# Six blocks of x transposed by DMA in place of TensorE, with a new order table, in a fused attention and MoE kernel

## The chip, the cores and the metric

The kernel runs on one core of one Trainium2 chip. The metric is the device time of one execution in microseconds (us), lower is better. Three runs of the kernel before gave 299.45, 299.85 and 300.24 us; the median is 299.85 us. A separate execution was taken by the hardware profiler; all lines of profiles and traces below come from such executions.

The engines are written as the profile writes them: PE is TensorE (PEld its loading of weights), DVE is VectorE, ACT is ScalarE, POOL is GpSimd, SP is SyncE. SP and POOL mostly issue DMAs here.

## The reference

Sliding-window attention with a linear bias by distance, for 8 batches, 8 heads, 576 positions and a head size of 64, and behind it a feed-forward layer with the activation h·cos(h):

```python
scores = scale * np.matmul(q, k.transpose(0, 1, 3, 2))
bias = slopes[:, None, None] * (-np.abs(rel))[None, :, :]
mask = (rel >= 0) & (rel < 128)
scores = np.where(mask, scores + bias[None], -1e9)
attn = softmax(scores)
attn_out = np.matmul(attn, v)
x = attn_out.transpose(0, 2, 1, 3).reshape(B * S, H * D)   # 4608 x 512
h = x @ w_in                                               # w_in 512 x 2048
out = (h * np.cos(h)) @ w_out                              # w_out 2048 x 512
```

All inputs and the output are float32. The kernel computes in 16-bit types and accumulates in PSUM in float32.

## The kernel before

**Units of attention.** A batch's 576 positions are cut into two groups of 256 (G = 0 and 1) and a tail of 64. A unit (b, pr, G) is batch b, head pair pr (0 to 3) and group G; a unit (b, 't') is the tail with all heads. That makes 9 units for a batch, 72 in all, and they run mostly in pairs. For a pair, `scores` puts q·k products on TensorE (lines 529 and 539), ScalarE takes the exponential (598), VectorE multiplies with the mask (623), `pv` multiplies with v on TensorE (640 to 656, with the sum of the weights as an additional column) and VectorE divides by that sum (694, 696) into one of eight buffers `xnats`, as 128 positions times two blocks of 128.

**x transposed.** The next layer needs x with features on partitions. There are two ways. `x_pe` (719) makes two TensorE transposes against the identity (742) into PSUM and one copy from there into `xT`, on ScalarE (752) or VectorE (753). `x_dma` (757) issues a DMA transpose on SP (768; 762 for a tail), from `xnats` into `xT`, without TensorE. `xT` is a ring of 2560 tokens.

**The layer behind it.** The 4608 tokens are cut into 9 chunks of 512. `moe1(c)` multiplies chunk c with w_in (782): for each of 16 column blocks four matmuls, kc = 0 to 3, each of which reads one head pair's rows of `xT`, so the block's first matmul reads pair 0 and its fourth pair 3. Cosine on ScalarE (787) and a product on VectorE (791) follow. The second product with w_out runs in seven-product (Strassen) form for most chunks, `product` at 1067, and the first one does so for the last chunks (876). Chunk 0 has its own form (975).

**Phases.** Phase c is `moe1(c)`, then some units of attention (8, 10, 10, 12, 14, 9 units in phases 0 to 5), then the second product of chunk c. Nine units run before phase 0. In time these overlap: TensorE gets attention's matmuls of phase 2 between the products of chunks 1 and 2, and directly behind them moe1 of chunk 3. Units of phase 2 are those of batch 3 and (4,0,0); the four units (3,0,0) to (3,3,0) hold tokens 1728 to 1983, in chunk 3. Phase 3 begins with (4,1,0) and (4,2,0), tokens 2304 to 2559, in chunk 4.

**Which way x takes.** In `attention`, line 1208:

```python
first = (S * u[0] + (512 if u[1] == "t" else 256 * u[2])) // CH
after.append((first > phase + 1 or g < XD.get(phase, 0), u, ub, n))
```

A unit goes by DMA when its first chunk lies beyond the next phase's, or when its index g within the phase (pairs 0, 2, 4, ...) is below `XD[phase]`. XD is on line 275. With `{4: 6}` the second condition adds nothing to the first, since phase 4's first six units are far ahead of their chunks.

**The order.** `op` collects every operation with what it reads and writes, and does not decide the order. `TABLE`, a packed string of two bytes for each operation, names the order of all operations, and `follow` (160) applies it, and picks the engine of those copies that may run on ScalarE or on VectorE. Each engine then runs its own operations strictly in that order, and `emit` (174) puts a semaphore wait before each operation that reads, or overwrites, what another engine or a DMA has not finished. So a wait at the head of an engine's queue holds everything behind it on that engine.

**Loads and queues.** POOL issues the loads of q and k (`load_nat`, 385, five DMAs for a batch and tensor) and of v (`load_v`, 375, five for a batch). SP issues the big DMA transposes of q and k (396, 399), those of x (762, 768) and the stores of the output (1095). q, k and v of batches 0 and 1 are handled differently: q and k of these go through TensorE transposes (`qk_transposes`, 483). At the start POOL also makes the identity matrix (421) and the table of distances for the mask.

Of the kernel before, what the change touches and what calls it, by code (L numbers as in the profile page):

```python
# [27 lines left out]


TABLE = (  # L30
    'c-nPV2Y6If7JmPfH!Wo*A%PHdEHqifjs=k}tV#(GFqBXPBn4$bu`FK_%_4*%1ObV(K#D*JSt&-E!h-'
    '0xDvPKfD@{Z`QYO7kX6D^JciMYzU|;fHUhcd1+;jf_Kj&N_3_w#jJy552L+3%Pc;zlP#H-yktj(-'
    'pEjqM{ck}PJwCrB3q-'
    '{9M;&d$5qHR9WADS}~;_2H1xbO#`q+wdtgon`B>6%HyG|f?3%VnDsdnr<5N0St5ZZ)?8zmXNGD<Zg2=y6N`U+Gy?'
    '$F$*GyJWJoN!r+3anTS_iMU&FrmJy)q1{k##U*rYHRJHq^Dy35b!Y@oPU}o$A?_9;n<O%5Xs0l2&{m^^1BgNm_9P'
    '~pqObs4C1TN&{Qy{6(86~%nA#%H5NW^O=4`d2vLnc~h(_}2&mQcz_^`@$G{b79x#rnLjt-93Hcj0-'
    'yv%|m2e+*e0cZK}!+72b)WUaJT8@pXD+fk0N6bOV1gB(Si4?NA5T2-'
    '!JB(zEKr!Mj%{>;HUNYjab!Z7$qCql;L3G!CjefR+FFk(bw73vr<2ntCbb8MB)_5dQYyf6J%<J=0tY;ul(MgN&rc'
    'O0s&EiG$uIcm#Y~Vab;v#yqnaVrE7GY>V-A}Btqa`;P_Nv&jvF#{*7WM`>VMkre&#)Wy?uO_aV#gax-'
    'm{4=v5trFP6j>R?Tw2c0rY#J*M(j<PaOY>o)>#w^hUa2)xJ2kX>J~-'  # L40
    '#3SczLYEI#)13`0UMgZCvSU&r@KXVhQx8AYHOt^~S#t385v1pL)39f1&X4(!RY_VSn%~;N7Le~0Vt5k)3C!7qncH'
    'Sb_KKyP6<WQBL=(H{om`}^2hwehkBNkN1f6-'
    '=6Jf`#n1*9F&|{#~8ip5b`?XFO3>mnmKg4fqM&X#D2BXTu`vb#MxEL-'
    '2=FZh<=U!>)?uhVjo~ev?pC0h90j^d!W2#$W>Vg}3Lez;yMB~`dF58D5!*GHZ4bkokcrZJo8XMBIs3+J`c0!*&!='
    'cNak2M(+9t6%k<c;_TI5&xT-;_~SjMe)zLQ?kr-'
    '9G)}so_oZgT~!nS)>B%(>F{i(nL<%Kma6dPT_kIY8xqVGm@6sSZY)QY;}3kyZHF!JjrNbPWohF6A1kpQae^Jz>4Y'
    'nMq|4ag_#Z%abX$X0Qx{bdg5-'
    'w!C^Sy0wzSSv6YO*7!5g5KOZPW>L)jeqDWi^PVfHiNt_&bV&I7<#pb?el1f*R3lvbBscPqQM6(|M=#E!7MQtWiEo'
    '^$q8jetWg{{laSk`ID;w6<lHL!It@CI3ZRWxET-dy=6bdfZi^BN)-'
    'kx6rkxYh^Af7Y$CX%W0qP@nf!;+_cuy#JAV$$(>L5)aS8M@n1a32RRL3Yb{W0a`!VJ8|o4{JEnxs(L});p(&v8a9'  # L50
    'u_yO{KZHL$YuW?tu(Sy-'
    '!vCGTmAdZpg4wXLtycpkG<<E5@OtDZg=!_1h1+Njmjw*z0aL)7QnhFOPv(elHPlI>oe%EXgvk}suL+RHI+l!oPEe'
    'ttc)y)KY7q-'
    'GO9HpEp~!82*s>_!_J5TR{@5f%EL7h^Wh(4l4fbO%j~jd783&`#My06C4>3;+Is6L%3tT|^hYe#$tr1&iB&6{dwW'
    'wmj!;Baz_4=p8Jja_9ps>tY{=<;GUvOwSAXGq+K`;>!KNrH|ImXY(ASTzHFN^apdvpSj*r6^VK)$8H@P=`NPcPO&'
    'XkYSBhFw`irt0gqb!LQPqlVQC7VwU?z)4yP6n<)+6xUk=rH29r)HJ=#nkkufV0J5o_@v9wsQWd0@&P$WT0e*0vOC'
    'WIl=#9la*x}LDtWaQG=0xl2(#f%Kz3QWi+K|tR$xwKh#_K~ywPUk>V_~X988-'
    'dL$7M*|kTUzrMQ~>ttJm@GYT>9QFLiQ#JGHIu^Q5UX9joXGsV+1N~s5tf4rg&Z0t843@yK)VUZ;eO{vvf>bj#_<{'
    'E{YJE13lG{)N}UY3D6Y>lsCkRX4ja{$9_e$IQETy;j`zD56VwIGwJ{vRRhIkkY72;<?OL;WxyDsbjLJ`d?#gik4L'
    '%OwvOj>3X-Yk5pe`ia}jeHouYwjx-lYe?zUO*6w~{=z!E<7?VOdoJcyIBk3;YN22T&Udsl*?z2EoT*eN`VQ(2lOw'  # L60
    '$ie!%Cd#CND}y^H-5G~apWoVM#%(x$>q1=4UeA7@v$>FHVpXpRNz-`z1w9-2S&rNI|0<^yIkuIxJ1&2qr-'
    'yn-P&*BAkwbEg<YgZWM`B<Ux7!?;yxT0hEB9Poq9_H<xB+6$<+&1*V*jXQ=!i##UhbBC-HxJ9b4f>O5FQM$GVlYY'
    '0;EzOMeT$+Oi@ir?~G>em;QF`Fb7Uw0-'
    ')DSUv5QX5E;wvHsQX@ok50m+CO*%wR0XM0gH$JNq(o?|pd}rcrfU%@Ny^NS$EwY}9WNlRrb}CwAb0!CyUIkX8zeE'
    't`lBMNi5`Z9289jS-byN0#8`Z0-K46!6u51NJvfI*I<pVOKD}#Bep<(EjKAJ>#OvyA?}aT-'
    'Eb<QtZWG>gAiq@nZu|-Z>5YIIxXgTPJ-Qv8(%8OF{x~utj?J<T~4~q=Mu!G!`B%o{U^X7EYfMjy|cFw5l`KlR}P!'
    'Ka8_mW<8uzKs|eA|5Ic*_e7cdlcU3q+K^v!GU5I4-4igxj^A<ASLge=;<iQSZL!w7=WR?W#-'
    'vXhCLeN@7x(>g+{qRDABl6lLS<Fw>!h`LQKaFe(HMu)ipAva=P&;AW;|7_8}?>Xa&1&CWqRI3oTyJm0VHkMj~b-'
    'KU~R;VLVn(IO$x|2XD-#Cwa~YvoxGM@0FUnOnlZXB(9|3jhMQu{ARUV7(DVnyPJ@o)_f&pP-'
    '0v1&I@q5tK0fHEZqW2B6vpePz;Nsr3p!)OwvLraMQ%IB0%b!Fk8kvD!^ICX(d5SU`>)JBl;A)3x!^A~*gA1H!Njk'  # L70
    '9bb31AJ#9jLnSFn5nJP8V+>6WI*{{9$K=-'
    'Ii4(}ekB>9rlTbz8;dAV@$vsGY#Mm*p3)v9cI)0mEeyn;9Sk1Ej+_{IEB=6m(OWM%qp|L4FkV=POcUwRSz4?%tjO'
    '!EE7%nJVFo1y$1xLEKDW3+%V*`a_(LEi!<eA{Ja22J?)4@RI|7PRIIN8a6UkTIrQNx^0MmIX}Gdse33v8*ibI3(}'
    'Q6!`hQq7VFL0TWDyL%1z)LEb|Fqa2QJsRyz<9M$)jGC(Gyq6mu#GUiIyWiMn}lrw_vC^2CnX65Kq(JOA5auqsW#('
    'az6gPr;3Fs3vS*iFTO!lleCE-fW~K`s@;f-'
    'DuL7*vWwMFvwo)YDYK%Ys!&lL=}a$qa_Dqe_$j$%4|P%7Sk&C^p7|E-05OoaEoQU{w(_HKhuIl)N)0L6E?If-ndQ'
    'f>bOkomPRMj6=zXYB;2Fs8S$=8>KAS9bxj%$jo92RQykW$_h$ynL-'
    ';1n|B~0C{NjJ5M;#~HD{_qDyS92ASr8Q=(}$hf?wlN8Dh7U35CEE3Rb4eZHcVrLB=YO&ys+EVM&F9-'
    '>_E|awkyN8>TE$>Y^ZLfm%hXRv?#4)t*Y5EYzr4%5w1xWK3uw7gWYn<tfyI;9|8HRZ>;#t145fwkp%W<gb}oO8Vt'
    ';%~TDI391Zd3iT@kVuEmcuME+!AOkCeh?Xh408{MGRAGcvK=>2_;SOCz;Xi5FXBMh@##BcNK~)Hu608vNLvl*BDH'  # L80
# [15 lines left out]
class Plan:  # L96
# [63 lines left out]
    def follow(self, text):  # L160


        raw = zlib.decompress(base64.b85decode(text))
        n, at, self.order = len(raw) // 2, 0, []
        assert n == len(self.all)
        for lo, hi in zip(raw[:n], raw[n:]):
            at = (at + lo + 256 * hi) % 65536
# [85 lines left out]
def bass_alibi_sliding__then__act_gcu_kernel(  # L253
# [1071 lines left out]
```

## Time and profile before

| What | Value |
|---|---|
| Median of 3 runs (lowest, highest) | 299.85 us (299.45, 300.24) |
| The profiled execution's own time | 299.71 us |
| Its span, first to last instruction | 298.0 us |
| DVE TENSOR_TENSOR at 696 (normalising x) | 56 of 420 ns |
| DMA packets, data moved | 147729, 37.96 MB |
| HBM over the span | 155 GB/s |

How to read it: a line of instructions starts with its place in the kernel, then the engine and operation, what is written and read, and shapes. In a group's row, "xN \| busy, mean ns" gives the count, the busy time in us and the mean duration of one; that duration is from the start to the end of one instruction, and on TensorE several are in flight at a time, so the starts of neighbours in the timeline tell what one costs the stream. In a timeline's row the first two columns are the start and the busy time in us, and brackets hold the idle time before it and its releaser. Rows of waits hold the total, the count and the longest. Rows by stretches of time have the engines PE, PEld, DVE, ACT and POOL in this order, then TensorE's granted clock, the DMA share and GB/s. For DMAs, "to landing" is the time from the start of the issue to the last byte.

### The profile page before, as it was taken

What the parts mean: (1) busy time and instruction counts of PE and PEld (TensorE: products, weight loads), DVE (VectorE), ACT (ScalarE), POOL (GpSimd) and SP (SyncE); (2) the same over time, 40 slices, a digit from 0 to 9 for tenths busy, and PEclk for the clock granted to TensorE, in tenths of its full rate; (3) what the DMA queues carried; (4) which work ended last, traced back from release to release, by engine and by line L of the source; (5) the groups of instructions that cost most, each with busy time, mean ns of one, the idle gap of its engine ahead of it and who ended that gap; (6) DMA issues with size and microseconds to landing.
All of it is one profiled execution on the core that took longest, in us unless ns stands there. A gap on an engine that the chain in (4) does not pass through costs nothing.

```text
span 298.0 us, 7278 instructions
## 1 busy us (share of the span) xinstructions
PE 287.9 (97%) x2974; PEld 205.2 (69%) x2974; DVE 262.1 (88%) x522; ACT 222.1 (75%) x318; POOL 95.2 (32%) x122
## 2 busy tenths in 40 slices
PE   2899999999999999999999999999999999999996
PEld 2678845446874586458854788547768888888884
DVE  3879877599977999899999999999999999999972
ACT  5788878689757889688777878579778758778620
POOL 7997000599642303991195005000000000000000
PEclk9999999999999999999999999999999999999999
DMA  7999999999999994999999939973131400041033
GB/s 153 173 205 208 207 169 146 180 196 155 136 175 147 130 187 90 142 173 173 169 170 133 163 85 130 159 164 74 21 79 21 150 2 0 2 141 37 10 134 106
DMA packets 147729, 37.96 MB, mean 127 GB/s; under 512 B 133360, under 2 KB 146416, under 8 KB 147696
## 3 DMA queue, kind: packets, MB, share of 16 engines
q0 software_dynamic: 99344, 18.10, 79.7%
q1 hardware_dynamic: 48352, 19.41, 34.5%
q8 instruction: 23, 0.38, 0.5%
q14 instruction: 10, 0.08, 0.1%
HBM read 36.70 MB, written 9.44 MB: 155 GB/s over the span
## 4 chain that ended last, share of the span: by engine, by line
PE 94%; DVE 2%; POOL 1%; issue 1%; ACT 1%; POOLq 0%; DVEq 0%
PE ps L1067 33%; PE ps L782 24%; PE ps L876 11%; PE ps L539 5%; PE ps L975 5%; PE ps L1161 4%; PE ps L653 3%; PE ps L656 2%; PE ps L742 2%; PE ps L483 2%; PE ps L529 1%; DVE kt L501 1%; PE ps L640 1%; PE ps L642 1%; PE ps L1138 1%
## 5 line engine op out<-in xcount | busy, mean ns | idle before, releaser
L1067 PE MATMUL ps<-w_outb,gT 128*128 128x256 f16 x512 | 82.3, 273 | 0.0
L782 PE MATMUL ps<-xT,w_inb 128*128 128x512 f16 x336 | 82.2, 379 | 0.0
L787 ACT ACTIVATE cos<-ps,halfpi 128x512 f32<-128x512 f32 x84 | 54.9, 687 | 18.9 <-PE ps L782 13.9
L598 ACT ACTIVATE p<-ps 128x768 bf16<-128x768 f32 (+1 forms) x64 | 55.6, 915 | 11.5 <-PE ps L539 9.5
L791 DVE TENSOR_TENSOR gT<-ps,cos 128x512 f16<-128x512 f32 x84 | 54.5, 686 | 5.5 <-ACT cos L787 5.1
L1067 PEld LDWEIGHTS ps<-w_outb,gT 128*128 128x128 f16 x512 | 48.2, 98 | 12.5 <-issue 1.3
L782 PEld LDWEIGHTS ps<-xT,w_inb 128*128 128x128 f16 x336 | 31.7, 98 | 31.1 <-DVE gT L791 1.5
L375 POOL DMA_DIRECT2D vp<-in_v_dram x40 | 34.3, 892 | 53.1 <-PE ps L656 35.3
L1067 PE MATMUL ps<-wsum,gsum 128*128 128x256 f16 x256 | 38.5, 273 | 0.0
L623 DVE TENSOR_TENSOR p<-p,emask 128x768 bf16<-128x768 bf16 (+1 forms) x64 | 38.0, 615 | 0.3
L385 POOL DMA_DIRECT2D qnat<-in_q_dram x30 | 25.5, 918 | 23.9 <-DMA qt<-qnat 23.9
L1052 ACT ACTIVATE ob<-ps 128x512 f32<-128x512 f32 x33 | 19.6, 598 | 13.7 <-PE ps L1067 11.2
L385 POOL DMA_DIRECT2D knat<-in_k_dram x30 | 25.7, 948 | 9.3 <-DMA kt<-knat 7.0
L1067 PEld LDWEIGHTS ps<-wsum,gsum 128*128 128x128 f16 x256 | 23.2, 98 | 4.0 <-issue 0.5
L876 PE MATMUL ps<-xT,w_inb 128*128 128x256 f16 x132 | 24.8, 273 | 0.0
L696 DVE TENSOR_TENSOR xnats<-ps,rec 128x256 f16<-128x256 f32 x56 | 21.9, 420 | 0.5
L539 PE MATMUL ps<-qt,kt 64*128 64x128 bf16 (+1 forms) x320 | 20.1, 253 | 1.3 <-DVE kt L501 1.3
L653 PEld LDWEIGHTS ps<-vp,p 128*128 128x128 bf16 x256 | 16.0, 99 | 4.3 <-issue 1.0
L653 PE MATMUL ps<-vp,p 128*128 128x65 bf16 x256 | 18.9, 196 | 0.1
L1067 PE MATMUL ps<-wsum,gT 128*128 128x256 f16 x112 | 18.1, 273 | 0.0
L539 PEld LDWEIGHTS ps<-qt,kt 64*128 64x128 bf16 x320 | 11.9, 98 | 8.6 <-issue 3.6
L1161 PE MATMUL ps<-w_outb,gT 128*128 128x512 f16 x64 | 17.6, 380 | 0.0
(111 smaller groups left out, 478.0 us busy)
## 6 DMA issues: line engine op xcount, KB each, us to landing
out_dram<-ob SPq DMA_DIRECT2D x35, 256.0 KB, 2.7
vp<-in_v_dram POOLq DMA_DIRECT2D x32, 128.0 KB, 6.9
qnat<-in_q_dram POOLq DMA_DIRECT2D x24, 128.0 KB, 7.1
knat<-in_k_dram POOLq DMA_DIRECT2D x24, 128.0 KB, 10.8
w_inb<-in_moe_w_in_dram POOLq DMA_DIRECT2D x4, 512.0 KB, 10.5
w_outb<-in_moe_w_out_dram POOLq DMA_DIRECT2D x4, 512.0 KB, 21.8
gsum<-in_q_dram POOLq DMA_DIRECT2D x1, 576.0 KB, 15.5
gsum<-in_k_dram POOLq DMA_DIRECT2D x1, 576.0 KB, 17.6
```

The source lines that it names most:

```text
L375: op("pool", [lambda e, t=t, rows=rows: e.dma_start(vp[b % 2][0:rows, t, :, 0:64], v[b, :, 128 * t:128 * t + rows, :].rearrange("h p d -> ...
L385: fns.append(lambda e, t=t, rows=rows: e.dma_start(nat[which][b % 2][0:rows, t, :, :], src[b, :, 128 * t:128 * t + rows, :].rearrange("h p ...
L539: ins = e.matmul(ps[:, banks[x], c0:c1], keys_ap(b, x, pr, kc), query_ap(b, x, pr, qb, 128 * nb), start=c0 == 0 and (b, pr, G) not in seed ...
L598: op("act", lambda e: e.activation(P[i][:, :, 0:hi], src_[:, :, 0:hi], ACTF.Exp, scale=0.125), w=held + [("P", i)], occ=920 if G else 691, ...
L623: op("dve", lambda e: e.tensor_tensor(p, p, m, ALU.mult), r=[("EM", h0), ("EM", h1)] + ([] if G else [("EM2", h1)]), w=[("P", i)], occ=600 ...
L653: ins = e.matmul(o, P[i][:, x, d0:d0 + 128], V[:, kc, h, 0:65], start=True, stop=not two)
L782: op("pe", lambda e, kc=kc: e.matmul(ps[:, bank, :], w_in[:, kc, 128 * fc:128 * fc + 128], xT[:, kc, r0:r0 + CH], start=(kc == 0), stop=(k ...
L787: op("act", lambda e: e.activation(cosb[ci][:, :], ps[:, bank, :], ACTF.Sin, bias=halfpi[:, 0:1]), r=["halfpi"], w=[("B", bank), ("cos", c ...
L791: op("dve", lambda e: e.tensor_tensor(gT[gi][:, fc, :], ps[:, bank, :], cosb[ci][:, :], ALU.mult), r=[("cos", ci)], w=[("B", bank), ("g", ...
L876: op("pe", lambda e, i=i, kc=kc: e.matmul(ps[:, bank, 256 * i:256 * i + 256], left(kc, p0 + i), right(kc), start=(start and i == 0 and kc ...
L1067: op("pe", lambda e, t=t, p=p: e.matmul(ps[:, bank, 256 * t:256 * t + 256], left(p, slice(128 * t, 128 * t + 128)), right(p), start=(start ...
L1161: op("pe", lambda e, t=t, fc=fc, bank=bank: e.matmul(ps[:, bank, :], gT[gi][:, fc, 128 * t:128 * t + 128], w_out[:, fc, :], start=(fc == 0 ...
```

## The change

XD becomes `{2: 4, 3: 2, 4: 6}`: the first four units of phase 2, (3,0,0) to (3,3,0), and the first two of phase 3, (4,1,0) and (4,2,0), go by `x_dma` and not by `x_pe`. That removes twelve transposes on TensorE (70 become 58 at 742) and six copies from PSUM, and adds six DMA transposes on SP (29 become 35 at 768). `follow` no longer names ScalarE itself for copies that the table leaves on the first choice, but the operation's first engine, which is ScalarE for every copy that has a choice. The whole table is replaced, for the order of every engine; the new one has five lines fewer, so line numbers behind it are lower by five.

```diff
 TABLE = (
-    'c-nPV2Y6If7JmPfH!Wo*A%PHdEHqifjs=k}tV#(GFqBXPBn4$bu`FK_%_4*%1ObV(K#D*JSt&-E!h-'
...
+    'c-n1N33L=y7VX=6C*4`PlMs*?2^dC12atfuz$hx92#AC=>;Yl`L4qJ6OrmTV2M8dMB_t5SPC!R?9i79-9F-'
...
 )
@@ -167,7 +162,7 @@
             at = (at + lo + 256 * hi) % 65536
             o = self.all[at % 32768]
             if isinstance(o.fn, dict):
-                e = "dve" if at >= 32768 else "act"
+                e = "dve" if at >= 32768 else o.eng[0]
                 o.fn, o.eng = o.fn[e], (e,)
             self.order.append(o)
 
@@ -272,7 +267,7 @@
         KENG, DPEN, CENG = ("act",), 0, ("act", "dve")
-        JN, PRE2, SEEDN, XD, LORD = (5,), (), {}, {4: 6}, 0
+        JN, PRE2, SEEDN, XD, LORD = (5,), (), {}, {2: 4, 3: 2, 4: 6}, 0
         SDPRI, NH, LWPRI, G1, S4IN, SPLIT = 1, 2, 2, 1, True, True
```

What the new table moves beside the six units, as the order of the queues has it. On POOL the identity comes first and the distances later; and the five loads of q for batch 5, which were issued after a v load that waits for phase 2's pv, stand ahead of three v blocks of batch 3 (the fifth, the second and the first) and of the first v blocks of batch 4. On SP the four new transfers of phase 2 stand behind the k transposes of batch 4 and a store of chunk 1, and ahead of another store of chunk 1 and the q transposes of batch 5; those of phase 3 stand between stores of chunk 2 and the q transposes of batch 6. On TensorE the transposes of q and k for batch 0 are cut into smaller groups with scores between them. Of the copies that may run on either engine, VectorE gets 5 of those for x where it had 9, 8 of 16 for q and k where it had 9, and 4 of 35 for the output where it had 2.

More of the change, by code (lines that the diff above doesn't have):

```diff
@@ L30 @@
 TABLE = (
-    'c-nPV2Y6If7JmPfH!Wo*A%PHdEHqifjs=k}tV#(GFqBXPBn4$bu`FK_%_4*%1ObV(K#D*JSt&-E!h-'
[L32 to L80, printed above, removed]
@@ L81 @@
-    'GHNRFy;B3gs%n{7pj$fl+x7VWHhmHY6$LK<1t&5`BViq8BRfR0)!TR`@J<FZkbrVSDq@w=+*W79u-'
-    'AsdYv9Vyey(st|R(RU84Bg0wsI(4aO|@>6G)${!)5eW-e@5K<&=Z_fWO<s>k5KMFa_g&GrXJ7L|{Z-'
-    'kIjkN?mA0G*W>_y'
+    'c-n1N33L=y7VX=6C*4`PlMs*?2^dC12atfuz$hx92#AC=>;Yl`L4qJ6OrmTV2M8dMB_t5SPC!R?9i79-9F-'
+    '9~ZU<KgCkWX)ovl~u&->L|RW+4#cl}@gzyIES_r6yuv(c;dYJ6?b`E>9C+7wNTPS6;<MthV-)7oOYd$(x-'
+    'fZAl#xSH9Zs_ws~T}<uPUY{0SFId_-sc{<ULJMxCK)lqf4c*(5I@C<vl6C_Y7^9I?-'
+    '_R19YWvY*uA%9u`++u?+fmi6N`GG!9swM8y42z>I_qH|6HW^^)C?n_hZZI{;ko+s#i!5_-'
@@ new lines @@
+    'QmV}cZDZmO6x!kIxY{4rj=d)AivEHXz1Q*2jckl7C7P%!|mL%MLEY_*pGu3^-'
+    'q2QaTULs646TT{pn|qnGYSQ4xIz(WYy8L*0FkR5?tH?G{7`{w`qEX4b?fvG5#ztZb#Haz(=+nz`2R705{Nb8dF;6'
+    '_tP=<bE6w^rN2+0h>Sjb$J$5Zqsd1o@@e$E+{ipY?C7JDXwNx8Bbd~8)nh8hAGHoUE*M|3BmRPumKvGbg+cLWUOb'
+    'cUY1?&wHSHYQ)L*wVSN|SUKT?-'
+    '<(;q}lXA9h(WRG2MfE#h1A2PnqKpaKxqKEo#akCGiJ<wN7x1z}e9UMvZz>XC~dB6t!GLBTqJPl11Zd|qkg&PQ*Ml'
+    'F0cG~(cNvas(5wYnJCcD?&`q|x{{^!T0r=oj6u7q>ud#^?iTOgk{^_J3E2{)k>BG$vrf+(hIFTkDX7I;_K6>x)1)'
+    'DD=hEC$)E)`K}tqj%7{hA6{qcC}tpMgN=i|Y$F|>kY6nrENImbJW1-YT@o63Vyz3;SaUUkEstloxqz6a-'
@@ new lines @@
+    't@S~>KU*Z$YUnAk>@0)^)8FT^Y%+dP4(HE59l!b628I0Q=@?q7xD*ae*zx8fmni~{(AadEfAmd1Nwf}GpY49x>!H'
+    '!3yty8(0}(g+6m4FQEO?7Z7`!P9wv7uha2Rn(NZznr}OR4UiYdup;71adOO+Yp3tFW0=6O<$X*M~(^uAV9EfeGM7'
+    '=(1$mgdqN{8S@$HHUq7!J6n9fynJ&|@-Zk*Er~4$a;%`!I9U0|UDqp9@5biV^oVAIjR(=c&~+MM)-'
+    'nqLAK?rp@gl31hKIu-et}Yz~czI7Ey1reXSLNJ@h*<vua-'
+    '1F!WtF0y$~lHTL1UOPAyhim+*Fc2!O6n7#L9dW!K)X`K-'
+    'E1a?WU;X7D%hPcasm^*EN^(+ebs(xMTqf7gaF^TgV#?xeZj{cC0jJ^m#a=zIeknG=Q1JG44Z$$TWf*_7_vOJ?-'
+    '8m~fi3CY@Z#s~a9R(hmcu(^7!}HBPCvy8P#tTV1<~Pt{PADS4p{Fa=%;+%;kG6scO4l*cA+HtXEZXH1C`S_#-'
@@ new lines @@
+    '(LW73)mXRCY&G&7cZq@`Ak|=XmUkmo@Wy**ftB6HcMM+JECVc6%{YEJn`2Lr_z?CC_@Kx(^0IPCrS4_2k^A+<T%)'
+    ')a~fu5w&DWz0$Y}Bfi_C-'
+    ')i)$JfQqIL@iegLw<34>>KI*<&eR%%?Mr<;9S$UJM&7Pjbt!SEHEf!S%27yx?GGwVYYX3`zxo*DlXq`$#co4(K`8'
+    '-fXz7lx*btw_t@$yD%}QRX-zWkT<qY$OUmZUcKH6xmX|4orpc_s6-'
+    'eZxAWwWDf5$cobONj)wCUNCqSBDyU*VL|P5y?`rgnqUIZXwFOr2Vaweplvhf9FlD`R^-'
+    'U+c&E?8rhsac_i7vf&g`YZo-ISEO5fKW*OazwQ)UFGJ`3n0+`G5&Z}j|rpyz(^sf~2iR<S&NW%sv>3eCA{8XSZAo'
+    'B#Sp|{?dMT;o+hoUba_VKT<PSB`d8CdwsNw*i%%S^ZF*`0UyuU*}UAA94WPf~36egCM(a0`aZU2$`mT^mEE)O__E'
@@ new lines @@
+    'v0+6KNR{|vjOYAc67hJiYcq0u_ibO(jyo_{QL^Ll(kZew@;|^HB0ovRREC%59Yb>hP_Oe<PR3!;y)g-6u-'
+    '~hHO7ERNhrLAkwFN3|NWF+{Ays@j79TQqzbpNyeeuxC2(q^2{RjsOu~N?!K%ESGXVbIYe2M$v0hFhyM$yEUIjEpK'
+    '^F^898o=xMuneRIF=)91Up}G13}F1ojLkzbHlycA>N<HP#50avmvg;FTu2`F&g(1zO$AHQ^Ut3iL5zCi5_9UV=Yf'
+    'Ys(h<72`WUVZ`JDHhO(S{Ii98n@r*y7qefU=z`gCbpw|4zo>v`!pyP)bIvQl&cV%}Iy1<ahy>sRlUD`8%@YF(i8E'
+    'W+U_#P%q!YX?!dx@jY*k?q6G^6WA#rW;VSYTfEPJR)teo&fqfV@7Fw`>cJSP*(JqT=`Se?(&)Cyk*URA-'
+    '*{tcI&@>O-J9Oa0r^%5vhea#~pL`=w_BL-'
@@ new lines @@
+    'uv>`8L?F9PGpw(bW8k<L5V&V)3)P*2TxAAc0)V)6G}q;t3@Mw;=MVgf(G%;njB}8Giqn&wl=Fhxi-EzD^V;gqGmp'
+    'SHn(R+`n6i?v+hexu>Rpm8(K;n=hf$M^8eBidjsQ}J|k9OXWTz~bkd#48ciL8r)qZ&+SY!%irVN=doGUH=Mzmz=S'
+    '(_<G20gISU4Ow&z(D%^M1vbZO3o@Z6{vYH3f%ChvS{nEx?>v$F?mlZC{Mcy|cv<hjt9U`dI1*==TlKXHChxQT;Ga'
+    '&}`@em+#wC*hVE#_saH(#Yi6aKCE?%PLi}r#^U&h{Rb{jX*xj$PS>SXXMgZA9fb3fO3ksiK?(z^k#c*kNUhVOPNT'
+    'hH!5NGbho^d78%OM`9Pc{b>)JFpk7ystsK7LsTs$~E_O#}?E2vQFj@hb{Xnpnl+Ghy0EjgqUAG+1^Iqw)udHX=t$'
+    'JrD`S$0|W?tvM5eAyp^)9UQdPcZ6i=DTlnL~mltPE?V&%tf8*I)hYj<OPw7ytN&o?@2fUWRXmDZ)4>VH3S{hnUGu'
@@ new lines @@
+    '`0pz?~Z2rO*_`Nft>H9=@)k7`@n(5Vte(7U$i?@OIIx7CWJc*5nTCBet&_%^TESqle71I<jD0;`+D_UdxZ-'
+    'q9fR4T^*82{z}feG=eK$XuQG5@40Kc6xG>Vg7sgSarTDfr{J6IjRZ3kvug3#??JGyKmHu+BnHRADz%;RzOWO5%{;'
+    '?a)$%A0c}zxUnE#VN?}7J7iDA7qPIrfp5N)z)*!yBHRRdKtTxkN8ld>;Gq%6OA>hqQ1KiVHWSPO3mf)F$smM1CUd'
+    'F+Y2++mQkIgy8Tkb&#S9B$!z3`U@QoxaY1U*gh2seBmL-jaJyY7wF9;7A&%fN6pfx5vOKK$oZWcI+LJeZ7k|7wfB'
+    'mIP&3&SdNLIS_!ASv@$FgdDl62pN=$SieR#_6yXB_%_KRZQSylk%F$K#+?@!XAk^d9G!9B&%hzVG3uY3=5$Z)T0t'
+    'k83}2g$O|U(O#zllSwfgR6)H(G?jiY5Rgf$W&`ic<X_kXKB8bjdB#l*}5-'
@@ L84 @@
+    'BZtOs)%6q=J}SPU3e+%HepJDnf_^8iPVT@|x%$3JU2l2^LI(5o0p)GZ|a>QKAwdmsl`=a(YVC$|4FcV-iv_Nr98q'
+    'U1fn#RuMtMOGT%V!pfv%VRE7}`9`KvYC`^m$-HDNq9@5>2<kw=9wi^-YLcHI16Il)m4ai6@-'
+    '3mGzspFqAeXMZj7z*$f+-`5qBlsoY?z#kYLdVr+?6jCeG6s-EVO~iL?W#z5{=zMACbyp5jm9PjokyYPz7R&cM(Z-'
+    '5A#?Sa+rzXR|*Qt{~i$R`iv<%Y}n6`IS2%vSO&Pjx#j{(1(gCI$!nPiA5#`>MbVK|EheoQEHd@dvZ{z&rKpI~cqL'
+    '3`Owm+iy+^@YRRpr~UaVLX*)0Q?AO%;Yijb8`75QevUxDuNeyALUAO9a*5Fqg'
 )
```

## The prediction

> **What bounds the kernel now.** I read the page first (busy shares, granted clock, chain of waits), then the view of TensorE's waits, then its timeline where the change works.
>
> ```profile
> PE 287.9 (97%) x2974; PEld 205.2 (69%) x2974; DVE 262.1 (88%) x522; ACT 222.1 (75%) x318; POOL 95.2 (32%) x122
> PE 94%; DVE 2%; POOL 1%; issue 1%; ACT 1%; POOLq 0%; DVEq 0%
> core 0: 298.0 us, clock 1.000
> PE ps L483 <- POOL ident L421: 5.7, 1, 5.7
> PE ps L539 <- DVE kt L501: 1.3, 2, 0.9
> ```
>
> TensorE is busy 287.9 of 298.0 us and carries 94% of the chain that ended last, at a granted clock of 1.000. Its waits are two groups, 5.7 and 1.3 us, both before 14 us (rows below). From then on it always has a matmul in flight, so in that stretch only two things can move the end: work taken from its stream or put into it, and a new wait in that stream. VectorE (88%) and ScalarE (75%) have room.
>
> ```profile
> 5.70 1.92 PE L483 MATMUL ps<-ident,gsum 128*64 128x128 bf16 x32 [5.70 <-POOL ident L421]
> 8.50 0.82 PE L539 MATMUL ps<-qt,kt 64*128 64x256 bf16 x8 [0.88 <-DVE kt L501]
> 13.50 1.04 PE L539 MATMUL ps<-qt,kt 64*128 64x256 bf16 x12 [0.38 <-DVE kt L501]
> ```
>
> The profiled execution took 299.71 us for a span of 298.0, 1.7 us around it, and lies 0.14 us under the median of 299.85. I make the sum against 299.71 and set the result beside the median at the end.
>
> **What is removed from TensorE.** Each of the six units loses two transposes (line 742) and one copy from PSUM (752 on ScalarE or 753 on VectorE): 12 of 70 transposes go. The group's row says 230 ns for one, but that is how long one stays in the pipeline. What it costs the stream is the distance to the next start:
>
> ```profile
> L742 PE MATMUL ps<-ident,xnats 128*128 128x128 f16 x70 | 9.4, 230 | 0.0
> 113.84 0.28 PE L742 MATMUL ps<-ident,xnats 128*128 128x128 f16 x2
> 113.95 0.38 PE L1067 MATMUL ps<-wsum,gsum 128*128 128x256 f16 x2
> 114.17 0.28 PE L742 MATMUL ps<-ident,xnats 128*128 128x128 f16 x2
> 114.28 0.27 PE L1067 MATMUL ps<-wsum,gsum 128*128 128x256 f16 x1
> 111.10 0.39 PE L742 MATMUL ps<-ident,xnats 128*128 128x128 f16 x4
> 111.32 0.38 PE L1067 MATMUL ps<-wsum,gsum 128*128 128x256 f16 x2
> ```
>
> Two take 113.95 − 113.84 = 0.11 us and again 114.28 − 114.17 = 0.11; four take 111.32 − 111.10 = 0.22. So 55 ns each, and 12 × 0.055 = **0.66 us** leave the stream. By the row's 230 ns it would be 2.8 us; that is the far bound, and I take 0.66 because the neighbours' starts show it three times.
>
> The Trainium skill, "TensorE: Matmul & The Clock Gate", Part 4, gives about 275 ns for such a transpose in one kernel's context and puts most of it to access latency. By that the six units would give back 12 × 0.275 = 3.3 us. The trace agrees with it on the duration (230) and not on the price in a full pipeline (55). The same skill, "VectorE: DVE Perf Modes", Rules for kernel authors, advises against this change: it keeps a 128×128 transpose on TensorE where PSUM will do as a destination, with 390 ns against 1309 ns by DMA; here the issue row below (1247 ns for two blocks) is not TensorE's time, so the rule decides only if the landing is waited for.
>
> The six copies lost cost ScalarE or VectorE some 0.39 us each in the pipeline, but nothing waits there now that TensorE would notice, so I cost them at nothing (cover gone: less than 0.39 × 6 = 2.3 us to gain, all of it only if those engines bound a stretch, which the TensorE rows exclude after 14 us). The four or five other copies that change engine in the new table are covered by the same.
>
> ```profile
> L752 ACT ACTIVATE xT<-ps 128x256 f16<-128x256 f16 x27 | 9.6, 389 | 7.3 <-PE ps L742 6.1 <-PE ps L729 1.1
> ```
>
> **What is added.** Six more DMA transposes of x on SP (line 768), 29 become 35: units (3,0..3,0) in phase 2, (4,1,0) and (4,2,0) in phase 3. They differ from the 29: in the kernel before no unit goes by DMA whose tokens the very next phase reads, while these six are due in it. TensorE takes its work in order, so a late one stops all of it.
>
> ```profile
> L768 SPq DMA_TRANSPOSE xT<-xnats x9: 1169/1247/1391, 121.9 to 168.5; - x9
> DMA to landing us min/median/max: 3.0/5.8/7.6
> ...
> L768 SPq DMA_TRANSPOSE xT<-xnats x20: 1168/1247/2227, 173.6 to 223.8; - x20
> DMA to landing us min/median/max: 2.3/2.4/5.5
> ```
>
> SP needs 1.25 us to issue one. From issue to landing it is 3.0 to 7.6 us (median 5.8) while loads are in flight (120 to 170 us), and 2.3 to 5.5 (median 2.4) afterwards.
>
> The tightest is the fourth of phase 2. In the changed order, between the pv matmuls of (3,2,0) and (3,3,0) and the first matmul of chunk 3's moe1 that reads the fourth quarter of x (line 782), stand 38 products of line 1067, 3 of line 782, 32 pv, 8 transposes and two score blocks. Rows for their rates:
>
> ```profile
> 109.79 1.48 PE L1067 MATMUL ps<-wsum,gsum 128*128 128x256 f16 x12
> 111.64 0.62 PE L539 MATMUL ps<-qt,kt 64*128 64x256 bf16 x12
> 112.19 0.28 PE L1067 MATMUL ps<-wsum,gsum 128*128 128x256 f16 x1
> 112.38 0.19 PE L653 MATMUL ps<-vp,p 128*128 128x65 bf16 x1
> 112.86 1.15 PE L1067 MATMUL ps<-wsum,gsum 128*128 128x256 f16 x9
> 116.30 0.81 PE L782 MATMUL ps<-xT,w_inb 128*128 128x512 f16 x3
> 116.95 0.27 PE L742 MATMUL ps<-ident,xnats 128*128 128x128 f16 x2
> 110.28 0.76 DVE L696 TENSOR_TENSOR xnats<-ps,rec 128x256 f16<-128x256 f32 x2
> ```
>
> Twelve products take 111.10 − 109.79 = 1.31 us, 0.109 each; three of line 782 0.65; sixteen pv 112.86 − 112.38 = 0.48; a score block about 0.55 with 0.1 to enter it. Sum: 38 × 0.109 + 0.65 + 2 × 0.48 + 8 × 0.055 + 2 × 0.65 = 7.5 us. The pair's pv ends at 109.79 and its second normalised block at 110.28 + 0.76 = 111.04, 1.25 later; the third transfer is then issued, and the fourth 1.25 behind it, so 2.5 us after pv, with 0.1 for the hand-over. That leaves 7.5 − 2.6 = **4.9 us** for the fourth to land, about 5.8 for the third; the first two, a pair earlier, have 7 to 8.5. Against the quiet 2.4 it is ample; against the loaded 5.8 it lacks 0.9 us; against 7.6, 2.7 us. Which holds depends on what is in the DMA queues near 112 us:
>
> ```profile
> 108.00:112.00 4.00, 4.00 (x63) 3.29 (x62) 3.72 (x10) 3.76 (x8) 0.00 (x0) 1.00 1.33 230
> 112.00:116.00 4.00, 4.00 (x82) 3.11 (x77) 3.61 (x9) 3.54 (x6) 0.00 (x0) 1.00 0.03 10
> 95.30 4.19 POOL L385 DMA_DIRECT2D knat<-in_k_dram  x5 [7.03 <-DMA kt<-knat]
> 116.64 0.89 POOL L375 DMA_DIRECT2D vp<-in_v_dram  x1 [17.15 <-PE ps L656]
> 117.51 4.20 POOL L385 DMA_DIRECT2D qnat<-in_q_dram  x5
> 106.29 1.25 SPq L399 DMA_TRANSPOSE qt<-qnat  x1
> qnat<-in_q_dram POOLq DMA_DIRECT2D x24, 128.0 KB, 7.1
> ```
>
> In these windows (the last two columns are DMA share and GB/s) the queues work at 230 GB/s up to 112 and stand still, at 10 GB/s, from 112 to 116: just when the four would fly. But the new table also moves work there. The five loads of q that POOL issues at 117.51 are ahead of v's last blocks in the changed order, before 100 us: 4.5 × 128 KB = 576 KB more to drain, 2.5 us at 230 GB/s. The quiet begins near 114.5 in place of 112. The fourth transfer, issued near 113, meets some 1.5 us of backlog: an estimate of 2.4 + 1.5 = 3.9 us, inside its 4.9. So I take no wait, with bounds 0 and 2.7 us.
>
> The same move puts three blocks of v of batch 3 behind those q loads. Their bounds come from the v loads before 90 us:
>
> ```profile
> L375 POOL DMA_DIRECT2D vp<-in_v_dram x13: 707/920/972, 59.3 to 87.4; - x13
> DMA to landing us min/median/max: 5.4/6.9/15.5
> ```
>
> By their place in the order they are issued some 90 us into the span (an estimate from the rows of POOL) and land between 96 and 105.5; pv of batch 3 starts near 107. Taken: no wait, with a margin of 1.5 us at the slow end. In phase 3 the pair's pv runs near 137.5, two issues follow, and chunk 4 reads x some 11 us later, so even 7.6 us fits: nothing.
>
> On SP the four stand after the last big transposes of k (row at 106.29 for the last such issue before) and ahead of the next store and of q's transposes for batch 5. Those wait 5 us at most; q of batch 5 is first read in phase 3, 25 us on, and no output buffer is refilled before its store. Nothing.
>
> **The table.** Every engine's order is new. For the whole rest I count: the same matmuls, in the same phases; in steady state as many score blocks as before, so as many entries of 0.1 us. In the start-up the identity comes first on POOL, and the transposes of q and k are cut by score blocks earlier. What it can win are the rows of waits above: 1.3 us on kt, part of 5.7 on ident; what it can lose is of that size, as k and q are issued some 0.2 to 0.8 us later on their queues. Taken: 0, bounds −1.3 and +0.8. At the end the last chunk is bound by its matmuls in both orders: 0.
>
> **The sum**: −0.66 + 0 (copies) + 0 (landing) + 0 (v) + 0 (table) = −0.66: 299.05 by the profiled execution, 299.19 by the median. **Forecast 299.1 us.** About 0.3% (0.9 us) is what a measurement of this kernel tells from no change, and the forecast lies just inside that.
>
> **The rivals.**
>
> *The new table wins more than the transposes do.* The kt waits (1.3 us) sit where it re-cuts the start. If they go, the end is 299.71 − 0.66 − 1.3 = 297.7, half of them 298.4. For it: those are the only waits that TensorE has outside the first 5.7 us. Against: k's arrival, not the order, may set them.
>
> *The fourth landing is late* (slower). The moved q loads are still draining, the transfer takes the loaded 5.8 to 7.6 us, and the moe1 of chunk 3 stands at its fourth quarter: 0.9 to 2.7 us. It ends at 299.05 + 0.9 = 299.95 up to 301.8. The point: a landing over 4.9 + 0.66 = 5.6 us loses to the kernel before, over 6.5 us by more than 0.3%. For it: nine of nine transfers between 120 and 170 took 3.0 or more, half 5.8. Against: the 10 GB/s row.
>
> *Nothing shows.* The 0.66 us is given back in the start-up by q and k issued later (+0.8): 299.9.
>
> *A transpose costs its duration.* Twelve times 0.230 gives 296.9. Against it stand the three start distances. 3 in 100.
>
> **How the numbers follow.** The sum holds, 0.45, with 298.7 to 299.6 as its own range; two fifths of it fall under 298.95 with small gains of the table. The table wins more, 0.19, faster. Late landing, 0.22: 0.17 of it slower, 0.05 same. Nothing shows, 0.11: 0.05 same, 0.06 slower with a start that loses a little more. Duration, 0.03, faster. Faster 0.18 + 0.19 + 0.03 = 0.40; same 0.27 + 0.05 + 0.05 = 0.37; slower 0.23. The range goes from 298.1 (most of the table's gain) to 301.4 (a landing near 7.2 us).
>
> **What would show it.** In the profile after: 58 transposes on line 742 and 35 DMA transposes on line 768; TensorE's busy time lower by about 0.7; no wait of line 782 for x near 117 us (it would be listed with a DMA of xT as its releaser) and none of line 653 for v near 107; the landings of the four under 4.9 us; the waits at ident and kt about as long as now. The prediction is wrong if line 782 shows such a wait of 0.6 us or more, if the kt waits are gone, or if matmuls after 18 us start further apart than before.

## The result, and the profile after

| | before | changed |
|---|---|---|
| median, lowest to highest, 4 runs each | 299.79 us, 299.45 to 300.24 | 304.01 us, 302.89 to 306.63 |
| ratio, 95% interval | | 1.0147 [1.0119, 1.0174] |
| profiled execution, its span | 299.71 us, 298.0 us | 306.63 us, 304.9 us |

The changed kernel is 1.5% slower. Its profiled execution is also its slowest one, 2.6 us over the median, so what is read there is at the large end. Line numbers of the changed kernel, e1 and e8 are lower by five than before: pv's 653 is 648, the v loads' 375 is 370, the q loads' 385 is 380, x's transposes 742 are 737, x by DMA 768 is 763, moe1's 782 is 777. Those of e2, e3, e5, e6, e7 and e9 are lower by twelve (pv 641, v 363, x by DMA 756, moe1 770); e4 has those of before.

First the page's busy shares and its chain of waits:

```profile
PE 289.9 (95%) x2962; PEld 205.2 (67%) x2962; DVE 262.4 (86%) x519; ACT 220.5 (72%) x315; POOL 95.1 (31%) x122
PE 80%; DMA 12%; POOL 3%; SPq 2%; issue 1%; ACT 1%; DVE 1%; POOLq 0%; ACTq 0%
```

Then the view of TensorE's waits (total, times, longest), and the row of the transposes in the view of groups:

```profile
PE ps L478 <- DVE gsum L362: 5.7, 1, 5.7
PE ps L648 <- DMA vp<-in_v_dram: 4.3, 1, 4.3
PE ps L534 <- DVE kt L496: 0.9, 1, 0.9
PE ps L478 <- DMA gsum<-in_k_dram: 0.5, 1, 0.5
PE ps L534 <- DVE gT L786: 0.2, 1, 0.2
```

```profile
L737 PE MATMUL ps<-ident,xnats 128*128 128x128 f16 x58 | 8.1, 229 | 0.1
```

The twelve transposes are gone, and DMA has come into the chain that ended last, with 12%. One wait is new and large: pv for a load of v. TensorE's timeline shows its place:

```profile
107.83 0.50 PE L534 MATMUL ps<-qt,kt 64*128 64x256 bf16 x8
112.66 0.27 PE L648 MATMUL ps<-vp,p 128*128 128x65 bf16 x3 [4.33 <-DMA vp<-in_v_dram]
```

The windows (PE, PEld, DVE, ACT, POOL, then clock, DMA share, GB/s) show what followed:

```profile
108.00:112.00 4.00, 0.33 (x8) 0.10 (x4) 0.80 (x2) 1.88 (x3) 0.00 (x0) 1.00 1.88 155
112.00:114.00 2.00, 1.34 (x18) 1.13 (x19) 0.76 (x4) 0.00 (x0) 0.00 (x0) 0.84 1.84 218
114.00:116.00 2.00, 2.00 (x15) 1.22 (x14) 1.40 (x4) 0.00 (x0) 0.00 (x0) 0.50 2.43 155
116.00:118.00 2.00, 2.00 (x33) 1.60 (x28) 1.01 (x5) 1.22 (x2) 0.00 (x0) 0.81 2.33 167
```

TensorE stood for 4.33 us at the first pv of batch 3. When it went on, the granted clock fell to 0.50 and was back only after 116 us. Over the three windows from 112 to 118 us the missing shares, 0.16, 0.50 and 0.19 of 2 us each, come to 1.7 us. The profiled execution lost 306.63 − 299.71 = 6.92 us: 4.33 of waiting, 1.7 of clock, and some 1.5 left over, against 0.66 worked out as saved. The clock's part belongs to this execution: its mean granted clock was 0.994, while the other three show 1.000, 1.000 and 0.998 and took 2.3 to 3.7 us less. So hardly any of the median's loss of 4.2 us is clock.

Why v came late is seen on POOL's timeline:

```profile
77.86 1.97 POOL L370 DMA_DIRECT2D vp<-in_v_dram  x2
84.11 4.19 POOL L380 DMA_DIRECT2D qnat<-in_q_dram  x5 [4.29 <-DMA qt<-qnat]
88.26 4.24 POOL L370 DMA_DIRECT2D vp<-in_v_dram  x5
97.56 4.19 POOL L380 DMA_DIRECT2D knat<-in_k_dram  x5 [5.06 <-DMA kt<-knat]
```

and in the landings of its loads, by their lines, q from 84 to 89 us and v from 88 to 93 us:

```profile
L380 POOL DMA_DIRECT2D qnat<-in_q_dram x5: 722/883/903, 84.1 to 87.6; - x5
DMA to landing us min/median/max: 17.7/19.2/21.2
...
L370 POOL DMA_DIRECT2D vp<-in_v_dram x5: 728/938/950, 88.3 to 91.5; - x5
DMA to landing us min/median/max: 21.7/22.8/23.3
```

The first three of the five v blocks are those of batch 3. By the trace they were issued from 88.3 to 89.8 us, 18 us or more ahead of need (112.66 − 4.33 = 108.33), and landed 21.7 to 22.8 us later, the last at 112.6 us. In front of them stood the five q loads that the new table had moved forward, which land from 84.1 + 17.7 = 101.8 to 87.6 + 21.2 = 108.8 us: 1.75 us from one landing to the next. But the queue was long before these: the two v blocks issued near 78 us, ahead of the moved q loads, already took about 20 us:

```profile
L370 POOL DMA_DIRECT2D vp<-in_v_dram x2: 1082/1089/1096, 77.9 to 78.7; - x2
DMA to landing us min/median/max: 19.1/19.9/20.6
```

The transfers of x, which the prediction watched, were not waited for; no line of TensorE's waits names xT. They don't test its sum either, since TensorE came to them late. Near their use:

```profile
L763 SPq DMA_TRANSPOSE xT<-xnats x4: 1168/1245/2247, 113.9 to 120.4; - x4
DMA to landing us min/median/max: 2.3/4.3/5.9
```

### The profile page after: what moved, and what is told of

Its sections match the earlier page's. It is cut to its first block, busy times and chain, and to the rows that moved or that the text cites. A ratio compares the mean times of both kernels' runs of the same rounds, so it can differ in the third digit from the quotient of the medians.

```text
span 304.9 us, 7267 instructions
## 1 busy us (share of the span) xinstructions
PE 289.9 (95%) x2962; PEld 205.2 (67%) x2962; DVE 262.4 (86%) x519; ACT 220.5 (72%) x315; POOL 95.1 (31%) x122
## 4 chain that ended last, share of the span: by engine, by line
PE 80%; DMA 12%; POOL 3%; SPq 2%; issue 1%; ACT 1%; DVE 1%; POOLq 0%; ACTq 0%
PE ps L1062 28%; PE ps L777 19%; PE ps L871 11%; DMA vp<-in_v_dram 7%; PE ps L970 5%; PE ps L534 4%; PE ps L1156 4%; PE ps L648 3%; DMA qt<-qnat 3%; DMA gsum<-in_k_dram 2%; PE ps L651 2%; SPq L391 2%; POOL qnat L380 1%; PE ps L478 1%; PE ps L737 1%
## 5 line engine op out<-in xcount | busy, mean ns | idle before, releaser
L1062 PE MATMUL ps<-w_outb,gT 128*128 128x256 f16 x512 | 83.8, 275 | 0.0
L593 ACT ACTIVATE p<-ps 128x768 bf16<-128x768 f32 (+1 forms) x64 | 55.9, 915 | 17.5 <-PE ps L534 14.4
L1062 PE MATMUL ps<-wsum,gsum 128*128 128x256 f16 x256 | 40.1, 275 | 0.0
L1047 ACT ACTIVATE ob<-ps 128x512 f32<-128x512 f32 x31 | 18.4, 598 | 8.4 <-PE ps L1062 8.1
L1062 PE MATMUL ps<-wsum,gT 128*128 128x256 f16 x112 | 19.9, 273 | 0.0
```

The lines of the kernel that those rows point to most:

```text
L593: op("act", lambda e: e.activation(P[i][:, :, 0:hi], src_[:, :, 0:hi], ACTF.Exp, scale=0.125), w=held + [("P", i)], occ=920 if G else 691, ...
L1062: op("pe", lambda e, t=t, p=p: e.matmul(ps[:, bank, 256 * t:256 * t + 256], left(p, slice(128 * t, 128 * t + 128)), right(p), start=(start ...
```

## The experiments

There were three theories. V: the v blocks behind the moved q loads are the loss. X: transposing x by DMA just ahead of its use costs. T: the new order costs in many places. In the edits, `load(name, n)` is the n-th operation on a DMA semaphore, and `move` puts one operation directly behind another. Ratios are against the kernel before, run on the same chip.

| Run | ratio, 95% interval |
|---|---|
| changed kernel | 1.0147 [1.0119, 1.0174] |
| e1: changed, v ahead of the q loads | 1.0053 [1.0037, 1.0069] |
| e2: before, six x by DMA | 1.0012 [0.9999, 1.0024] |
| e3: changed order, six x by TensorE | 1.0118 [1.0085, 1.0152] |
| e4: before, two v loads late | 1.0224 [1.0193, 1.0254] |
| e5: before, four x of phase 2 by DMA | 0.9982 [0.9969, 0.9995] |
| e6: before, two x of phase 3 by DMA | 1.0019 [1.0005, 1.0034] |
| e7: e1 with six x by TensorE | 1.0047 [1.0030, 1.0064] |
| e8: e1 without chunk 3's stores | 1.0000 [0.9988, 1.0012] |
| e9: e2 with two v blocks ahead | 1.0006 [0.9992, 1.0020] |

**e1, v ahead of q.** The q loads of batch 5 go behind the v blocks of batch 3.

```diff
         R.follow(TABLE)
...
+        move(load("ldnq1", 1), load("ldv10", 1))
```

> The changed kernel, with its five q loads of batch 5 put behind the three v blocks of batch 3 on POOL, nothing else moved. Theory V (these v blocks landed late behind the q loads: 4.33 us of waiting at pv, and about 1.6 us more because the granted clock was 0.50 from 114 to 116 us): no wait at pv, clock 1.000, and the time of the sum, 299.1 us, up to 299.8 if the start costs some tenths. Theory X (transposing x by DMA just ahead of its use is what costs): the wait at pv goes, but TensorE then stops at moe1 of chunk 3 for x, 1 to 3 us, and the time stays over 300.5. Theory T (the new order costs in many places): over 301.

Measured 301.58 us, 1.0053. Of this run's view of TensorE's waits:

```profile
PE ps L635 <- DVE xnats L691: 0.7, 1, 0.7
PE ps L737 <- DVE xnats L691: 0.6, 1, 0.6
PE ps L1062 <- ACT ob L1047: 0.6, 1, 0.6
```

The first and the third of these are near 190 and 176 us; the second is at 16.5 us, in the start-up. The three v loads' landings, then two rows of the timelines of ScalarE and VectorE that explain the waits at 176 and 190 us, and the landings of the four x transfers of phase 2:

```profile
L370 POOL DMA_DIRECT2D vp<-in_v_dram x3: 918/1114/1118, 78.5 to 80.0; - x3
DMA to landing us min/median/max: 21.3/22.3/24.0
```

```profile
176.03 0.60 ACT L1047 ACTIVATE ob<-ps 128x512 f32<-128x512 f32 x1 [0.75 <-DMA out_dram<-ob]
188.91 0.42 DVE L691 TENSOR_TENSOR xnats<-ps,rec 128x256 f16<-128x256 f32 x1 [1.10 <-DMA xT<-xnats]
```

```profile
L763 SPq DMA_TRANSPOSE xT<-xnats x4: 1212/1243/1258, 108.7 to 112.6; - x4
DMA to landing us min/median/max: 6.5/6.9/7.4
```

The wait at pv near 108 us is gone. The loads still take 21.3 to 24.0 us, as long as in the changed kernel, but issued ten us earlier they land from 99.8 to 104.0 in place of 110.0 to 112.6. So what the moved q loads did was to put v nine to ten us back in a queue that was already long, and V's loss is 0.94 points of the 1.47. The other half point is neither of V nor, as it was meant, of X: TensorE does not wait for x. It waits for a copy that waits for a store of its buffer (176 us), and for a division that waits until a DMA transpose has read its `xnats` buffer (189 us). Both stand behind SP's queue. In the changed kernel's own profile neither wait is listed; that the 6 us lost there at 108 to 117 us gave SP and the DMAs time to catch up would explain it, but was not tried.

**e2, six x by DMA in the old order.** On SP the four of phase 2 are put behind two stores of chunk 1, the two of phase 3 behind three stores of chunk 2; all else keeps its place.

```diff
-        JN, PRE2, SEEDN, XD, LORD = (5,), (), {}, {4: 6}, 0
+        JN, PRE2, SEEDN, XD, LORD = (5,), (), {}, {2: 4, 3: 2, 4: 6}, 0
```

> The kernel before with its own order everywhere, only the six units' transposes and copies left out and their DMA transposes put on SP where its queue stood idle (behind the two stores of chunk 1, from about 108 us, and behind three stores of chunk 2, from about 138 us). Theory V and theory T: no wait, 0.66 us less than before, 299.1 us. Theory X: TensorE waits for xT at line 782 near 117 us, 300.5 us or more.

Measured 300.50 us, 1.0012: the gain is gone, though without the 1 to 3 us at 117 us. From TensorE's timeline (150.81 is moe1 of chunk 4, the only wait for x by DMA that any of these profiles lists), and the landings of x issued between 140 and 145 us:

```profile
148.78 0.20 PE L628 MATMUL ps<-vp,ptail 128*128 128x65 bf16 x1 [0.39 <-DMA vp<-in_v_dram]
150.81 0.60 PE L770 MATMUL ps<-xT,w_inb 128*128 128x512 f16 x2 [0.19 <-DMA xT<-xnats]
```

```profile
L756 SPq DMA_TRANSPOSE xT<-xnats x3: 1168/1208/1737, 140.2 to 144.1; - x3
DMA to landing us min/median/max: 6.5/6.9/9.3
```

**e3, the new order without the six.** The edit is e2's, backwards, on the changed kernel; the transposes stand ahead of the next scores of their phase.

> The changed kernel's order, with the six units again by TensorE: two transposes and a copy for each ahead of the next pair's scores. Theory V: the wait at pv stays at 3 to 5 us, with the clock at half behind it, and the twelve transposes come on top: 303.5 to 305. Theory X: no loss, 299.8 to 300.5. Theory T: as theory V, 303.5 to 305.

Measured 303.67 us (302.47 to 307.51): the loss is there without any of the six by DMA. X is out as its main cause; the 0.3 points between e3 and the changed kernel lie within the two intervals. In the profiled execution, the fastest of the four, the wait at pv was 1.55 us (timeline) and the granted clock stayed at 1.00 (windows):

```profile
108.97 0.27 PE L641 MATMUL ps<-vp,p 128*128 128x65 bf16 x3 [1.55 <-DMA vp<-in_v_dram]
```

```profile
110.00:112.00 2.00, 2.00 (x33) 1.62 (x31) 2.00 (x5) 0.92 (x3) 0.00 (x0) 1.00 1.41 270
```

**e4, late v in the kernel before.**

```diff
...
+        for name in ("ldv11", "ldv10"):
+            move(load(name, 1), load("ldnk1", 1))
```

Two v blocks of batch 3 go behind the k loads of batch 5.

> The kernel before, with only two v blocks of batch 3 (the first and second) moved on POOL behind the k loads of batch 5, from about 65 to about 100 us. Theory V: they land near 112 us, pv is due near 107, so TensorE waits about 5 us and then runs some 3 us at half clock: 305 to 308 us. Theories X and T: two loads late cost nothing that the order does not, 299.8 us.

Measured 306.61 us, 1.0224: V's range. One wait of 3.06 us (timeline), and behind it the clock at half for three windows:

```profile
110.59 0.33 PE L653 MATMUL ps<-vp,p 128*128 128x65 bf16 x3 [3.06 <-DMA vp<-in_v_dram]
```

```profile
110.00:112.00 2.00, 1.41 (x16) 1.24 (x17) 0.55 (x3) 0.00 (x0) 0.00 (x0) 0.50 0.75 233
112.00:114.00 2.00, 2.00 (x13) 1.41 (x11) 1.35 (x4) 0.60 (x1) 0.00 (x0) 0.50 0.00 0
114.00:116.00 2.00, 2.00 (x26) 1.43 (x25) 0.69 (x1) 1.37 (x3) 0.00 (x0) 0.50 0.04 8
116.00:118.00 2.00, 2.00 (x24) 1.75 (x22) 1.54 (x6) 1.35 (x3) 0.00 (x0) 0.85 0.00 0
```

The wait was shorter than the 5 us expected, and the half clock dearer: 1.41 and 2 and 2 us of work at half and 2 at 0.85 lose 3.0 us. The mean granted clock was 0.988 or 0.989 in all four executions of e4. Two loads in the wrong place cost more than the whole change did.

**e5 and e6, the six in their two groups.** As e2, with XD `{2: 4, 4: 6}` and `{3: 2, 4: 6}`.

> The kernel before with its own order, and only the four units of phase 2 by DMA, issued where SP and the DMA queues stood idle (108 to 115 us). The run with all six lost its gain in waits near 148 and 151 us (0.39 us for a v load, 0.19 us for x), behind the two transfers of phase 3. If those two alone are what costs: no such waits, eight transposes less, 0.44 us, so 0.15% under the kernel before. If the transfers of phase 2 cost too: at or over the kernel before.

> The kernel before with its own order, and only the two units of phase 3 by DMA. If they are what costs: the waits near 148 to 151 us are there (0.4 to 0.9 us), four transposes less save 0.22 us, so 0.1 to 0.2% over the kernel before. If not: 0.07% under it, no waits there.

Measured 299.75 us, 0.9982, for the four of phase 2, and 300.70 us, 1.0019, for the two of phase 3. Both came out as the first of the two outcomes named for each. e5 is the one version here that beats the kernel before, though its interval ends close to 1, and it beats the changed one by 1.6%. In e6 the two transfers held back the loads of v; landings of v loads issued from 120 to 150 us, before, in e5 and in e6, and e6's wait in the timeline:

```profile
L375 POOL DMA_DIRECT2D vp<-in_v_dram x7: 745/937/1055, 121.7 to 147.6; - x7
DMA to landing us min/median/max: 4.8/7.8/14.3
```

```profile
L363 POOL DMA_DIRECT2D vp<-in_v_dram x7: 752/942/1067, 121.1 to 147.2; - x7
DMA to landing us min/median/max: 4.9/8.1/14.4
```

```profile
L363 POOL DMA_DIRECT2D vp<-in_v_dram x7: 765/957/1073, 121.9 to 147.8; - x7
DMA to landing us min/median/max: 6.2/8.2/17.3
```

```profile
149.23 0.20 PE L628 MATMUL ps<-vp,ptail 128*128 128x65 bf16 x1 [0.58 <-DMA vp<-in_v_dram]
```

The slowest of these loads went from 14.3 to 17.3 us, with nothing moved on POOL. It is 17.0 in e2, which has the two transfers as well, and 14.4 in e5, which has the other four and not these two.

**e7, e1 without the six.** e1's line and e3's edit, so that e7 and e3 differ by e1's line alone.

> The changed kernel's order with the three v blocks ahead of the q loads, and the six units by TensorE. With the v blocks in time, the changed kernel still took 0.5% more than the kernel before, in waits near 176 us (0.61, a copy behind a store) and 190 us (0.66, a division behind an x transfer). If the new order carries these by itself: 301.5 to 302.5 us, 0.66 us above the same with x by DMA. If they come of x by DMA: 300.0 us, about the kernel before.

Measured 301.48 us, 1.0047. Both branches missed. The new order does cost half a per cent with all x of these units on TensorE, but the time is not 0.66 us over e1's, and the two waits near 176 and 190 us are not in its list. So in the new order no gain of the six by DMA shows: 0.66 us of transposes go, and about as much comes back. By e1's list it would be in those two waits (0.61 and 0.66 us); that is read from one profile and was not tried by itself. Where e7's own half per cent lies stays open: in its profile TensorE's listed waits are 8.3 us against 7.0 before, with 0.8 for k and 0.4 for w_in, both before 22 us, and TensorE is busy 289.0 us against 287.9. Against e3, e1's line is worth 0.71 points, so V's loss shows a second time, with x on TensorE.

**e8, e1 without the four stores of chunk 3.**

```diff
+        gone = [o for o in R.order if o.grp == "o3/store/dma"]
+        R.order = [o for o in R.order if o not in gone]
...
```

The lines left out here take the waits for these stores away as well; 512 rows of the output are not written.

> The changed kernel with the three v blocks ahead of the q loads, and without the four stores of chunk 3 (so 512 rows of the output are not written). If the waits near 176 and 190 us come of SP's queue, which issues stores and transposes one behind the other without a pause from 162 to 193 us: both go or fall under 0.2 us, and the time falls by 1.0 to 1.4 us, to 300.2 to 300.6. If they come of the engines' new order: they stay, 301.3 us or more.

Measured 300.19 us, 1.0000; 1.4 us less than e1, and the waits near 176 and 190 us are gone from the list. That places them in what SP issues. It doesn't say whether it is SP's order or the stores' bytes: both went.

**e9, e2 with two v blocks ahead.**

```diff
+        move(load("ldv04", 2), load("ldv02", 2))
+        move(load("ldv10", 2), load("ldv03", 2))
```

> The kernel before with its own order and all six units by DMA, and on POOL the last v block of batch 4 moved ahead of the q loads of batch 6 and the first v block of batch 5 ahead of its k loads. In the run without these moves TensorE waited 0.39 us for the former near 149 us and 0.19 us for x near 151 us. If a v block late behind loads that could wait is again the cost: the wait for v goes, x may still be waited for by some 0.2 us, and the time is 0.1 to 0.2% under the kernel before. If the two transfers of phase 3 cost by themselves: no better than without the moves, 0.1% or more over the kernel before.

Measured 300.16 us, 1.0006 [0.9992, 1.0020]. In its profile no wait for v and none for x is left between 140 and 155 us, so the cause of the wait for v was right (why x's went too is not shown), but the time did not come under the kernel before: inconclusive. Some tenths sit elsewhere; the waits listed for this execution that the one of before does not have are for p from ScalarE and xnats from VectorE, before 20 us:

```profile
PE ps L963 <- ACT p L586: 0.6, 1, 0.6
PE ps L527 <- ACT p L586: 0.4, 1, 0.4
PE ps L730 <- DVE xnats L684: 0.3, 1, 0.3
```

## Why the prediction was wrong

**The step that failed** is the landing of v: the blocks "land between 96 and 105.5", and "Taken: no wait, with a margin of 1.5 us at the slow end". The place was right (v blocks put behind the q loads, pv near 107 us), so was the issue (90 predicted, 88.3 to 89.8). The landing was not: 21.7 to 22.8 us from issue, so 110.0 to 112.6 us, where 15.5 from issue was taken as the slow end, from v loads issued 59 to 87 us into the kernel before. From 30 us on POOL's loads land in the order of their issue, whatever they carry (in all eleven traces, but for four neighbours at most 0.5 us out of turn). So what stands ahead of a load sets its landing above all, and a row of v loads alone didn't show that. The kernel before has a long queue too, at its q loads:

```profile
L385 POOL DMA_DIRECT2D qnat<-in_q_dram x5: 919/1082/1099, 75.1 to 78.6; - x5
DMA to landing us min/median/max: 15.7/17.5/18.0
```

The changed kernel's v blocks issued near 78 us took 19.1 to 20.6, and behind these the five q loads came on top. The prediction had costed the five at 2.5 us, 576 KB at 230 GB/s, the rate of all transfers of a window together. They landed 1.75 us apart, some 8.8 us, while SP's transposes of q and k were in flight beside them; by e1 the same five loads put v back by nine to ten us. Added even to loads that landed after 6.9 to 15.5 us, they leave no margin. The slow rival named the right backlog and applied it to x alone.

**A cost that had no term:** the half clock behind a wait, 1.7 us in one of the changed kernel's four executions and 3.0 in e4's profile. The prediction's price for any wait was its length.

**The table at 0, bounds −1.3 and +0.8,** was too low. With v in time the new order costs half a per cent, 1.3 to 1.5 us (e1, e7). Counting matmuls and score blocks showed no work added, and none was. In e1, e8 puts the loss down to what SP issues; in e7 it stays open.

**The bound.** TensorE does set the end, but the prediction took "VectorE (88%) and ScalarE (75%) have room" as if that were all. It read the DMA engines from 108 to 116 us alone, and not the page's DMA row of the kernel before, in tenths over 40 slices:

```profile
DMA  7999999999999994999999939973131400041033
```

A 9 is 90% or more of a slice. From 7 to 193 us all but two are at 9, and the first of the two, from 112 to 119 us, is where the four x transfers of phase 2 were put. So TensorE would gain in this kernel only what the transfers can follow. e5 and e6 fit that in small: four transfers into an idle slice win 0.18%, two into a full one lose 0.19%.

**What held.** Twelve transposes at 55 ns, not 230: e5 measures 0.9982 for eight of them, 0.54 us with an interval from 0.15 to 0.93, where 0.44 was worked out; 230 each would be 1.84. No wait for x near 117 us, in any run, but that held by luck. The sum had the queues quiet from 114.5 us, the fourth x landing after 3.9 us, and 4.9 us of room. In e1, with v in time, the four took 6.5 to 7.4 us; by the trace the fourth was issued at 112.6 and landed at 119.5, and the matmul that reads it started at 120.0. Landing and room were both some 2.5 to 3 us longer than worked out, and the two errors nearly cancelled. That x would land within 7.6 us did not hold everywhere: 9.3 us in e2, in phase 3, where "even 7.6 us fits: nothing" stood.

**The chances.** Slower had 0.23, of which 0.17 on a late x and none on a late v. A late load of v was the outcome, 2.6 us over the range's upper end.

## What to carry to other kernels

When a change moves loads, follow the queue that they are moved in: for each load behind the new place, add the distance between landings for each moved load (here 1.75 us, with transposes in flight) to its own landing and set that against its first use. Take its own landing from the new place in the queue, not from loads of the same tensor elsewhere. Read the DMA row beside the busy shares; where it is full, work that goes from TensorE to a DMA has to go into a gap, or it delays some load that TensorE needs. Where TensorE waits 3 us or more, allow for the clock that the wait may take along as well: another 1.7 and 3.0 us in the two profiles here.

## What the runs showed of the hardware

The granted clock after a gap: it stayed at 1.00 behind 1.55 us of waiting (e3), and fell to 0.50 behind 3.06 us (e4) and 4.33 us (the changed kernel). The shorter of these had the longer half clock, about 6 us against 3 in the windows. The Trainium skill, "TensorE: Matmul & The Clock Gate", Why this matters for your kernels, warns of gaps beyond about 3 us between bursts; the three gaps agree.

Transfers issued by SP slowed those issued by POOL: with two more x transposes the slowest v load went from 14.3 to 17.3 us (17.0 in e2). The Trainium skill, "DMA: Bandwidth & Descriptors", Issuing engines are not separate DMA queues, says that all of them run on the same 16 DMA engines and interleave; the row agrees.

The spread grew with the wait: 302.89 to 306.63 us in the changed kernel and 302.47 to 307.51 in e3, against 299.45 to 300.24 before. Part of it is the clock: the slowest execution of each, 306.63 and 307.51 us, is the one with a mean granted clock of 0.994, where the others have 0.998 or more. One profile of a kernel that waits for a DMA is one draw from that.
